# A planner's table of offsets, keyed by stream, segment and share of the work done

## Chip, core, metric

One core of one Trainium2 chip. The metric is device time per execution in microseconds, the median of the runs. The granted TensorE clock is 1.00 over the whole profile.

## What is computed

Two transformer layers over 2048 tokens of width 640, all in bf16: attention with a compressive memory (32 heads of 20 features, four segments of 512 tokens), then a feed-forward part (FFN) with 1728 hidden features. The second layer uses the same weights. Cut to what matters:

```python
for s in range(N):                                   # N = 4 segments, L = 512
    p = softmax(einsum('bhqd,bhkd->bhqk', qs, ks) * scale + mask)
    a_dot = einsum('bhqk,bhkd->bhqd', p, vs)
    a_mem = (phi(qs) @ M) / (phi(qs) @ z + 1e-06)    # memory of earlier segments
    outs.append(g * a_mem + (1.0 - g) * a_dot)       # g = sigmoid(beta)
    M = M + phi(ks)^T @ vs;  z = z + phi(ks).sum()
...
x = x + A(layernorm(x));  x = x + relu(layernorm(x) @ w1) @ w2      # twice
```

## The kernel before

The work is cut into eight stages, segment 0 to 7: layer a and segment s make segment 4a + s. A segment needs its tokens normalised (`lnorm`), transposed by a DMA on SP's queue (`turn`, L745) and projected: keys and queries (`proj_part`, evicted at L910 or L911), values (L965). Keys and queries go to a DRAM scratch (`spill`, L999) and come back laid out by head (`fill`, L1046, four transfers for each pair of head groups) into one of four `pad` buffers. A pair m of head groups (four heads each) then has ten half-rounds of scores (L1230, PE in quarters of rows), taken two at a time, ten exponentials on ACT (L1292), the causal mask on POOL (L1304), the product with the values, and the division by the softmax sums (L1376 to L1418). In segment 0 the product with the values is made token by token (L1363, 40 small matmuls on the whole array); afterwards it runs in quarters of columns (`apply`, L1324), is evicted (L1334) and transposed (`turn_pair`). The memory is read (`mem_read`, L1110) and written (`mem_write`, L1167), its keys transposed by `turn_k`; the segment's output is added up (`combine`, L1437), transposed (`turn_o`), multiplied by wo (`out_proj`) and added to x (L1446), and the FFN follows (`ffn`, `ffn_rest`, evicted at L1528 or L1529, added at L1550).

There are eight PSUM banks. The scores use two slots of two banks, all other groups four single banks. Until the last scores of segment 0, two of those four are lent to the scores as a third slot.

**What sets the order.** Each engine runs its instructions in the order in which they were recorded, and so does each DMA queue. A planner (`Sched.run`) fixes this order when the kernel is built. Every piece of work is a generator, a "stream", with a number n by the order in which it was added: 0 scores, 1 exponentials, 2 masks, 3 value products, 5 `turn_pair`, 6 `divide`, 7 `turn_o`, 8 and 9 the halves of `out_proj`, 10 and 11 the second normalisation, 12 `fill`, 13 `spill`, 14 `combine`, 15 and 16 phi, 17 and 18 `mem_read`, 19 `turn_k`, 20 `mem_write`, 21 to 26 and 28 the first tiles, 27 `proj_ln`, 29 and 30 the key and query projections, 31 the values, 32 and 33 the FFN, 34 the stores, 35 to 38 constants and loads; evictions are streams of their own with higher numbers. The planner keeps a model of when each engine is free and each ticket due. At each step it takes, of the streams' next operations, the one with the smallest key: the start by its model, plus a lateness term, plus the stream's entry in `SHIFT` in nanoseconds (line 348); ties go by priority, segment and n:

```python
key = (round(start + late + SHIFT.get((n, self.rank[id(st[1])]), 0)), 0.5 if op.urgent else prio, self.rank[id(st[1])], n)
```

A negative entry has an operation recorded ahead of others that would start a little sooner, a positive one behind them. `rank` is the segment for the streams made by `each` and 0 for all others, among them the scores, exponentials, masks, value products, pair transposes and divisions (made by `items` or by themselves). A group of matmuls (`group`, L702 and L705) is recorded on the whole array (L702) or in four quarters of columns (L705); the planner chooses after each score pair (`_mode`), by whether a value product, which runs in quarters of columns alone, is due within 2500 ns of its model.

Of the kernel before, what the change touches and what calls it, by code (L numbers as in the profile page):

```python
# [13 lines left out]
NSEG = 4  # L14
# [4 lines left out]
G = H // 4  # L19
# [139 lines left out]
class Spawn:  # L159
# [31 lines left out]
class Sched:  # L191


    def __init__(self, prog):
# [9 lines left out]
        self.landed = set()  # L204

# [7 lines left out]
    def set(self, *key, tks=()):  # L213
        assert key not in self.events, key
        self.events[key] = [t for t in tks if t is not None]

# [95 lines left out]
    def run(self):  # L312
        while True:
# [24 lines left out]
            for prio, n, st, alts, op, late in heads:  # L338
# [9 lines left out]
                key = (round(start + late + SHIFT.get((n, self.rank[id(st[1])]), 0)), 0.5 if op.urgent else prio, self.rank[id(st[1])], n)  # L348
# [33 lines left out]
            else:  # L382
# [6 lines left out]
                out = marks[0] if len(marks) == 1 else (marks or None)  # L389
# [53 lines left out]
def bass_interleave_layers__memory_aug_infini_attn__dense_activation_relu__prompt_kernel(  # L443
    nc, A_x, A_wq, A_wk, A_wv, A_wo, A_beta, B_x, B_w1, B_w2, out,
):
    with contextlib.ExitStack() as es:
# [649 lines left out]
        def mem_read(hb):  # L1096
            def f(a, s):
# [35 lines left out]
                if len(READ[a, s]) == 2:  # L1133
                    for p in range(2):
                        PHS[p].release(*READ[a, s])
# [538 lines left out]
```

## Time and profile before

| | |
|---|---|
| median of 3 runs | 553.89 us (553.56 to 554.15) |
| span of the profiled execution | 552.1 us; the other 1.8 us of the median lie outside the first and last instruction |
| PE busy | 544.5 us, 9969 matmuls |
| DVE, ACT, POOL busy | 417.5, 413.0, 195.8 us |
| exponentials of segment 0 | 19.1 to 60.3 us |
| exponentials of segment 1 | 69.3 to 123.0 us |
| exponentials of segment 7 | 420.2 to 475.5 us |

The profile of one execution gives busy times by engine and by stretch, the waits by who ended them, the chain of work that ended last, and a timeline in which instructions of one kind in a row are merged (start, length, engine, line, tiles, count, and in brackets the idle time ahead of it and what ended it). Matmuls are pipelined and their ends are modelled, so PE can be shown busy while it starts nothing new; the time from one start to the next shows that.

### The profile page before, as it was taken

The numbers are of one execution on the slowest core, as the hardware profiler recorded it, in microseconds if no ns is written. First come the engines' busy times: TensorE is split into PE (matmuls) and PEld (weight loads), VectorE is DVE, ScalarE is ACT, GpSimd is POOL, SyncE is SP. The second block draws the span as 40 slices with busy tenths as digits, with TensorE's granted clock in tenths as the row PEclk, the third lists the DMA queues.
The fourth block names the chain that finished last, engine by engine and source line by source line (L and its number), as shares of the span: only waits on it lengthen the run. The fifth ranks groups of instructions, "written<-read, shape, count | busy, mean of one in ns | idle before, by whom it ended". The sixth has DMA issues, their size and how long they took to land.

```text
span 552.1 us, 22367 instructions
## 1 busy us (share of the span) xinstructions
PE 544.5 (99%) x9969; PEld 311.6 (56%) x9969; DVE 417.5 (76%) x1052; ACT 413.0 (75%) x531; POOL 195.8 (35%) x305
## 2 busy tenths in 40 slices
PE   8999999999999999999999999999999999999998
PEld 7554554455554555646456465654646654766656
DVE  4977899899798949987788759987968788745102
ACT  6699779889878878788888858888887779423140
POOL 5345334333344334443434404444333434201000
PEclk9999999999999999999999999999999999999999
DMA  8596989623861533953377841359138521433101
GB/s 266 147 224 179 195 202 209 195 78 66 170 146 44 78 68 100 151 98 69 62 143 151 136 147 45 69 97 136 23 103 174 93 50 29 96 63 62 40 2 51
DMA packets 130163, 61.52 MB, mean 111 GB/s; under 512 B 108948, under 2 KB 119956, under 8 KB 130068
## 3 DMA queue, kind: packets, MB, share of 16 engines
q1 hardware_dynamic: 129504, 59.57, 50.4%
q8 instruction: 78, 1.28, 0.9%
q10 hardware_dynamic: 564, 0.53, 0.4%
q14 instruction: 17, 0.14, 0.1%
HBM read 20.56 MB, written 12.85 MB: 61 GB/s over the span
## 4 chain that ended last, share of the span: by engine, by line
PE 88%; ACT 6%; DMA 2%; DVE 2%; SPq 1%; issue 0%
PE ps L705 43%; PE ps L702 27%; PE ps L1230 9%; PE ps L1324 6%; ACT PT L1292 5%; PE ps L1110 2%; DMA wq_r<-in_A_wq_dram 1%; PE ps L1504 1%; DMA pad<-scr 1%; PE ps L1167 1%; DMA pad<-stg 0%; ACT stg L1075 0%; SPq L1026 0%; DVE stats L723 0%; DVE o_sb L1418 0%
## 5 line engine op out<-in xcount | busy, mean ns | idle before, releaser
L1292 ACT ACTIVATE PT<-ps 128x1024 bf16<-128x1024 f32 x320 | 308.8, 1032 | 55.9 <-PE ps L1230 53.9
L1304 POOL TENSOR_SCALAR_AFFINE_SELECT PT<-PT 128x512 bf16<-128x512 bf16 x256 | 169.0, 678 | 250.2 <-ACT PT L1292 250.2
L705 PE MATMUL ps<-xnT,w_r 128*32 128x512 bf16 x1464 | 89.1, 380 | 0.0
L705 PE MATMUL ps<-w_r,hT 128*32 128x320 bf16 (+1 forms) x1868 | 71.2, 295 | 0.0
L1230 PE MATMUL ps<-pad 20*128 20x512 bf16 (+3 forms) x1024 | 63.4, 301 | 0.8 <-DMA pad<-scr 0.3
L1550 DVE TENSOR_TENSOR x_sb<-x_sb,ps 128x320 bf16<-128x320 bf16 (+1 forms) x65 | 30.9, 475 | 43.6 <-PE ps L705 39.9
L702 PE MATMUL ps<-w_r,hT 128*128 128x320 bf16 x378 | 62.4, 300 | 0.0
L723 DVE BATCH_NORM_STATS2 stats<-x_sb 128x6 f32<-128x320 bf16 x124 | 55.2, 478 | 3.2 <-DMA x_sb<-in_A_x_dram 2.6
L705 PEld LDWEIGHTS ps<-xnT,w_r 128*32 128x32 bf16 x1464 | 36.0, 97 | 33.6 <-issue 4.4
L705 PEld LDWEIGHTS ps<-w_r,hT 128*32 128x32 bf16 x1868 | 47.5, 97 | 12.7 <-issue 0.2
L1529 ACT ACTIVATE hT<-ps 128x512 bf16<-128x512 f32 x55 | 33.0, 599 | 21.1 <-PE ps L705 19.6
L1230 PEld LDWEIGHTS ps<-pad 20*128 20x128 bf16 x1024 | 17.9, 92 | 53.1 <-ACT PT L1292 26.9
L1446 DVE TENSOR_TENSOR x_sb<-x_sb,ps 128x320 bf16<-128x320 bf16 x64 | 30.5, 481 | 19.3 <-PE ps L705 15.1
L702 PEld LDWEIGHTS ps<-w_r,hT 128*128 128x128 bf16 x378 | 34.8, 98 | 18.2 <-issue 5.3
L1324 PE MATMUL ps<-PT,v_aug 128*21 128x128 bf16 (+3 forms) x896 | 40.3, 300 | 0.0
L910 DVE CAST stg<-ps 128x512 bf16<-128x512 f32 (+1 forms) x41 | 27.3, 668 | 16.6 <-PE ps L705 9.5
L739 POOL TENSOR_TENSOR rstd<-lnU,mhalf 128x2 f32<-128x2 f32 (+2 forms) x27 | 21.1, 781 | 50.9 <-DVE lnU L735 43.4
L1528 DVE TENSOR_SCALAR hT<-ps 128x512 bf16<-128x512 f32 x49 | 33.5, 685 | 7.3 <-PE ps L705 6.0
L702 PE MATMUL ps<-xnT,w_r 128*128 128x512 bf16 x154 | 37.4, 380 | 0.0
L705 PE MATMUL ps<-wo_r,oT 128*32 128x320 bf16 x864 | 36.7, 300 | 0.0
L1334 DVE CAST otu<-ps 128x512 bf16<-128x512 f32 x45 | 30.7, 682 | 5.5 <-PE ps L1324 4.2
L1075 ACT ACTIVATE stg<-stg 128x512 bf16<-128x512 bf16 x50 | 31.7, 636 | 1.2 <-DVE rtmp L1073 1.0
(114 smaller groups left out, 741.3 us busy)
## 6 DMA issues: line engine op xcount, KB each, us to landing
pad<-scr SPq DMA_DIRECT2D x124, 80.0 KB
scr<-stg SPq DMA_DIRECT2D x34, 256.0 KB, 2.8
out_dram<-x_sb SPq DMA_DIRECT2D x15, 160.0 KB, 2.8
w_r<-in_B_w_dram SPq DMA_DIRECT2D x10, 216.0 KB, 2.6
w_r<-in_B_w_dram SPq DMA_DIRECT2D x13, 160.0 KB, 2.8
x_sb<-in_A_x_dram SPq DMA_DIRECT2D x10, 160.0 KB, 3.0
scr<-w_r SPq DMA_DIRECT2D x5, 256.0 KB, 3.2
wv_r<-in_A_wv_dram SPq DMA_DIRECT2D x1, 800.0 KB, 9.7
```

The source lines that it names most:

```text
L702: return e.matmul(view(dst.ap, b), a, b, start=(k == 0), stop=(k == last))
L705: return e.matmul(view(dst.ap[rows], b), part, b, start=(k == 0), stop=(k == last))
L723: tk = yield dve(320, 1, lambda e, c2=c2: e.bn_stats(stats6[:, t, c2, :], x_sb[:, t, c2 * 320:(c2 + 1) * 320]), xt)
L1075: te = yield act(512, lambda e, q=q: e.activation(q, q, ACT.Exp), [tr] + p, psum=False)
L1230: fns.append([(lambda e, z=z, j=j, hh=hh, N=N, o=o, sl=sl, q=hh % 2: e.matmul(slot.ap[:, q, o:o + N], sl.ap[32 * hh:32 * hh + DH, z, 0, 12 ...
L1292: tx = yield act(1024, lambda e, dst=dst, src=src: e.activation(dst, src, ACT.Exp, scale=SCALE), sc + pw)
L1304: tm = yield pool(600.0, lambda e, reg=reg: e.affine_select(out=reg, in_=reg, pattern=[[0, 4], [1, 128]], compare_op=ALU.is_ge, fill=0.0, ...
L1324: fns.append((lambda e, OD, j=j, hh=hh: e.matmul(OD.ap[32 * hh:32 * hh + DH + 1, 128 * j:L], VAUG[vx(a, s)][:, j, 4 * g + hh, :], pt.ap[:, ...
L1334: te = yield evac(L, 1, lambda e: e.tensor_copy(dst, OD.ap), lambda e: e.activation(dst, OD.ap, ACT.Copy), [tk] + OTU[0].tks)
L1528: th = yield evac(512, 1, lambda e: e.tensor_scalar(hT[:, dc, :], bk.ap[:, :], 0.0, None, ALU.max), lambda e: e.activation(hT[:, dc, :], b ...
L1529: lambda e: e.activation(hT[:, dc, :], bk.ap[:, :], ACT.Relu), [tk] + HT.tks)
L1550: ta = yield dve(n, 1, lambda e: e.tensor_tensor(x_sb[:, t, c0:c0 + n], x_sb[:, t, c0:c0 + n], bk.ap[:, 0:n], ALU.add), [tk], urgent=True)
```

## The change

The table `SHIFT` is replaced. Its key becomes a triple: stream number, segment, and a share of the stream's work in this segment (0 below 6 recorded operations, 1 below 20, 2 below 60, 3 from there). So that the streams that had no segment get one, `items`, `scores` and `exps` now tell the planner when they enter a segment (`enter`), and each recorded operation of a stream is counted (`made`). Streams that never enter a segment stay in 0. Instead of 86 offsets there are 229. The lists that gathered tickets until both halves of a piece of work were recorded become one helper, `meet`, that releases the same buffers with the same tickets. `rank`, the tie-break and the operations stay as they were.

```diff
@@ -172,18 +172,44 @@
 PE_MARGIN = 80.0
 HOLDERS = 1
 SHIFT = {
-    (5, 0): -3000, (7, 0): -700, (7, 1): 400, (7, 2): -1000, (7, 4): 4300, (7, 5): -1100, (7, 6): -2700,
...
-    (18, 1): -200, (18, 2): -100, (18, 3): -200, (18, 7): -400, (19, 0): -1600, (19, 1): 100, (19, 4): -100,
-    (19, 5): -400, (19, 6): 1000, (20, 0): -200, (21, 0): 200, (22, 0): 100, (24, 0): 100, (26, 0): -100,
-    (27, 4): 200, (27, 5): 200, (27, 6): -100, (27, 7): -100, (29, 6): -100, (29, 7): -400, (30, 6): -400,
...
-    (33, 5): -1400, (33, 7): -200, (34, 4): -800, (34, 7): -200, (36, 0): 100, (37, 0): 1500, (38, 0): -300,
+    (0, 0, 0): -138, (0, 0, 1): -25, (1, 0, 0): 200, (1, 0, 1): 200, (1, 0, 2): 200, (1, 1, 0): 700, (1, 1, 1): 700,
+    (1, 1, 2): 700, (1, 2, 0): -275, (1, 2, 1): -225, (1, 2, 2): -100, (1, 3, 0): -925, (1, 3, 1): -925,
+    (1, 3, 2): -925, (1, 4, 0): 500, (1, 4, 1): 525, (1, 4, 2): 500, (1, 5, 0): -1888, (1, 5, 1): -1888,
+    (1, 5, 2): -1888, (1, 6, 0): 100, (1, 6, 1): 100, (1, 6, 2): 100, (1, 7, 0): -1450, (1, 7, 1): -1450,
+    (1, 7, 2): -1450, (2, 0, 0): 400, (2, 0, 1): 400, (2, 0, 2): 1000, (2, 2, 0): 300, (2, 2, 1): 300,
...
+    (7, 3, 0): -375, (7, 5, 0): 7775, (7, 7, 0): 4500, (8, 1, 0): -200, (8, 1, 1): -200, (8, 1, 2): -150,
...
+    (12, 3, 1): -500, (12, 5, 0): -1525, (12, 5, 1): -1525, (12, 6, 0): -25, (12, 6, 1): -25, (12, 7, 0): 4500,
+    (12, 7, 1): 4500, (13, 0, 0): -513, (13, 1, 0): -700, (13, 2, 0): -300, (13, 3, 0): 300, (13, 4, 0): -2000,
...
+    (19, 0, 0): -850, (19, 1, 0): 700, (19, 2, 0): 200, (19, 4, 0): -700, (19, 5, 0): 4250, (19, 6, 0): 375,
+    (20, 0, 0): -162, (20, 0, 1): -162, (20, 1, 0): 25, (20, 1, 1): -188, (20, 4, 0): -600, (20, 4, 1): -1225,
+    (20, 5, 0): -125, (20, 5, 1): -125, (21, 0, 0): -25, (21, 0, 1): 100, (22, 0, 0): 400, (24, 0, 0): 188,
...
+    (27, 6, 0): -62, (27, 6, 1): -62, (27, 7, 0): -2075, (27, 7, 1): -112, (29, 1, 2): 50, (29, 6, 0): -175,
...
+    (34, 7, 0): 400, (35, 0, 0): -300, (36, 0, 1): -650, (37, 0, 0): -100, (37, 0, 1): -100, (38, 0, 1): -25,
 }
 HOLD_TOL = {"pe": 220.0, "act": 150.0, "dve": 200.0, "pool": 0.0, "sp": 0.0}
 
@@ -202,6 +228,10 @@
         self.mode = "full"
         self.soon = 0.0
         self.landed = set()
+        self.met = {}
+        self.seen = {}
+        self.phase = {}
+        self.made = {}
 
     def add(self, prio, gen):
         self.streams.append([prio, gen, None, None, False])
@@ -213,6 +243,21 @@
     def set(self, *key, tks=()):
         assert key not in self.events, key
         self.events[key] = [t for t in tks if t is not None]
+
+    def enter(self, gen, phase):
+        if self.phase.get(id(gen)) != phase:
+            self.phase[id(gen)] = phase
+            self.made[id(gen)] = 0
+
+    def place(self, n, gen):
+        k = self.made.get(id(gen), 0)
+        return n, self.phase.get(id(gen), 0), sum(k >= x for x in (6, 20, 60))
+
+    def meet(self, key, count, tks, then):
+        self.met.setdefault(key, []).extend(tks)
+        self.seen[key] = self.seen.get(key, 0) + 1
+        if self.seen[key] == count:
+            then(self.met[key])
 
     def _fill(self, st):
         while st[2] is None and not st[4]:
@@ -345,7 +390,7 @@
                 if not ok:
                     continue
                 end, start, k = min(ok)
-                key = (round(start + late + SHIFT.get((n, self.rank[id(st[1])]), 0)), 0.5 if op.urgent else prio, self.rank[id(st[1])], n)
+                key = (round(start + late + SHIFT.get(self.place(n, st[1]), 0)), 0.5 if op.urgent else prio, self.rank[id(st[1])], n)
                 if best is None or key < best[0]:
                     best = (key, st, end, start, k, op)
             if best is None:
@@ -387,6 +432,7 @@
                         self.t[(id(tk[0]), tk[1])] = end + tail
                         marks.append(tk)
                 out = marks[0] if len(marks) == 1 else (marks or None)
+            self.made[id(st[1])] = self.made.get(id(st[1]), 0) + 1
             st[2], st[3] = None, ((slot, out) if slot is not None else out,)
 
 
...
@@ -1129,11 +1175,12 @@
                     bk.release(tm)
                     wr.append(tm)
                 S.set("omem", a, s, hb, tks=wr)
-                READ.setdefault((a, s), []).append(tk)
-                if len(READ[a, s]) == 2:
-                    for p in range(2):
-                        PHS[p].release(*READ[a, s])
-                    BDS.release(*READ[a, s])
+
+                def read(tks):
+                    for slot in PHS + [BDS]:
+                        slot.release(*tks)
+
+                S.meet(("read", a, s), 2, [tk], read)
             return f
 
         def turn_k(a, s):
@@ -1205,7 +1252,7 @@
 
         HALVES = [(m, u, k) for m in range(NSEG * G) for u in range(5) for k in range(2)]
 
-        def scores():
+        def scores(me):
 
             pads = {}
             LEND_FROM, LEND_TO = ("stg", 0, 0, 4, 1), ("sc", NSEG * 0 + G // 2 - 1, 4, 1)
@@ -1262,6 +1309,7 @@
                         for z in (a, b):
                             fns += z[2][y] if y < len(z[2]) else []
                     return pe(233.0, fns, a[1] + b[1] + a[0].tks + b[0].tks, take=[a[0], b[0]], mode="rows"), None
+                S.enter(me[0], HALVES[h][0] // (G // 2))
                 tks = yield Either(ask)
                 for tk, sl in zip(tks, list(took)):
                     m, u, k = HALVES[h]
@@ -1270,8 +1318,9 @@
                         pads[m].release(tk)
                     h += 1
 
-        def exps():
+        def exps(me):
             for m in range(NSEG * G):
+                S.enter(me[0], m // (G // 2))
                 pts = []
                 for u, parts in enumerate(ROUNDS):
                     if u in (0, 2):
...
@@ -1511,9 +1555,7 @@
                             lambda e: e.activation(hR[:], bk.ap[:, 0:L // 2], ACT.Relu), [tk] + HT.tks)
             bk.release(th)
             S.set("hR", b, s, tks=[th])
-            HALF[b, s] = tk
-            if (b, s, 0) in HALF:
-                xt.release(tk, HALF[b, s, 0])
+            S.meet(("half", b, s), 2, [tk], lambda tks: xt.release(*tks))
 
         def ffn(b, s):
             xtk = yield Need("hx", b, s)
...
@@ -1589,6 +1629,7 @@
             def g():
                 for a, s in AS:
                     S.rank[id(me)] = NSEG * a + s
+                    S.enter(me, NSEG * a + s)
                     if early is not None:
                         for st in S.streams:
                             if st[1] is me:
@@ -1598,11 +1639,17 @@
             return me
 
         def items(f, count):
-            for n in range(count):
-                yield from f(n)
-
-        S.add(0, scores())
-        S.add(0, exps())
+            def g():
+                for n in range(count):
+                    S.enter(me, 2 * NSEG * n // count)
+                    yield from f(n)
+            me = g()
+            return me
+
+        for f in (scores, exps):
+            me = []
+            me.append(f(me))
+            S.add(0, me[0])
         S.add(1, items(causal, NSEG * G))
         S.add(1, items(apply, 2 * NSEG * G))
         S.add(1, each(free_v))
```

More of the change, by code (lines that the diff above doesn't have):

```diff
@@ L807, in first_tile, with both @@
             S.set("turned0", t, tks=[tc])
-            FIRST.setdefault(t // 2, []).append((tc, tT))
-            if len(FIRST[t // 2]) == 2:
-                bx.release(*[x for _, x in FIRST[t // 2]])
-                S.set("xt", 0, 0, t // 2, tks=[x for x, _ in FIRST[t // 2]])
-        FIRST = {}
+            def both(tks):
+                bx.release(*tks[1::2])
+                S.set("xt", 0, 0, t // 2, tks=tks[0::2])
+            S.meet(("first", t // 2), 2, [tc, tT], both)
         PIECES = ((0, 1), (1, 2), (2, 4))
@@ L1091, in phi_ @@
             return f
-        READ = {}
         early_done = []
@@ L1456, in turn_o @@
                 ot = yield Acq([OT[k]])
-                ot.users = []
                 tT = yield from turn(ot_sem[id(ot)], ot.ap, o_sb[:, 2 * k:2 * k + 2, :].rearrange(
@@ L1474, in f @@
                     if i % 2:
-                        ot.users.append(tk)
-                        if len(ot.users) == 2:
-                            ot.release(*ot.users)
+                        S.meet(("ot", a, s, i), 2, [tk], lambda tks, ot=ot: ot.release(*tks))
             return f
@@ L1490, in ln_b @@
             return f
-        HALF = {}
         def ffn_rest(b, s):
@@ L1540, in ffn @@
                 yield Spawn(6, square(dc, bk, tk))
-            HALF[b, s, 0] = tk
-            if (b, s) in HALF:
-                xt.release(tk, HALF[b, s])
+            S.meet(("half", b, s), 2, [tk], lambda tks: xt.release(*tks))
             w2t = yield Need("w2")
```

32 rows, old and new, of the table SHIFT are left out of this document.

## The prediction

> **What bounds the kernel now.** I read the busy times by stretch first, then PE's timeline inside the stretches that have holes, then the other engines' timelines beside those holes. The stretches (columns: length; busy us and instructions of PE, PEld, DVE, ACT, POOL; granted clock; DMA share; GB/s):
>
> ```profile
> 0.00:20.00 20.00, 17.47 (x165) 13.67 (x166) 11.91 (x38) 11.02 (x27) 8.16 (x26) 1.00 0.67 204
> 20.00:40.00 20.00, 19.60 (x249) 10.81 (x248) 17.20 (x45) 18.97 (x25) 9.32 (x14) 1.00 0.86 221
> 40.00:60.00 20.00, 18.57 (x292) 9.31 (x288) 15.40 (x44) 19.95 (x23) 11.83 (x18) 1.00 0.72 188
> 60.00:80.00 20.00, 19.26 (x181) 11.32 (x180) 17.04 (x50) 13.89 (x21) 5.99 (x9) 1.00 0.89 193
> 80.00:120.00 40.00, 40.00 (x587) 19.02 (x583) 36.44 (x88) 36.03 (x45) 16.66 (x26) 1.00 0.74 179
> ...
> 480.00:520.00 40.00, 40.00 (x1055) 27.25 (x1046) 18.90 (x51) 8.14 (x14) 1.52 (x2) 1.00 0.29 63
> ```
>
> PE has no hole after 80 us (0.13 us idle up to 480) at clock 1.00, and its last matmul starts at 549.5 of a span of 552.1. So a microsecond PE loses anywhere is late at the end, one for one, and only PE's time can be won. Only ahead of 80 us does PE stand idle, and there ACT is nearly full (38.92 of 40 us between 20 and 60).
>
> "Busy" hides part of the loss, since matmuls overlap. So I sum start-to-start times of PE's matmuls. Inside a group they are 215.5 ns for 512 columns and 136 ns for 320: 192 columns more cost 79.5 ns, 2.4 columns per ns, plus 2.5 ns each. Four matmuls on 32 columns or 20 rows each start together and count once. From first to last start 548.4 us pass. Of this, 491.2 us are columns; 37 us are 326 changes between the shapes (whole array, quarters of columns, quarters of rows), each 96 to 113 ns by the medians of its kind; 160 score pairs bring two each. The rest is small steps, the first 20 us, and stalls above the usual step: **4.3 us between 20 and 80 us, 0.6 us after 80**. How a stall looks (PE, start, length):
>
> ```profile
> 44.86 0.40 PE L1230 MATMUL ps<-pad 20*128 20x256 bf16 x8
> 45.19 0.60 PE L702 MATMUL ps<-hT,wk_r 128*128 128x512 bf16 x2
> 46.01 0.60 PE L702 MATMUL ps<-hT,wk_r 128*128 128x512 bf16 x2 [0.22 <-DVE o_sb L1380]
> ...
> 51.08 1.04 PE L702 MATMUL ps<-hT,wk_r 128*128 128x512 bf16 x4 [0.40 <-DVE w_r L910]
> 52.11 0.40 PE L1230 MATMUL ps<-pad 20*128 20x384 bf16 x8
> 52.57 1.15 PE L1363 MATMUL ps<-w_r,PT 128*128 128x21 bf16 x40
> 53.58 0.38 PE L702 MATMUL ps<-hT,wk_r 128*128 128x512 bf16 x1
> 53.95 0.40 PE L1230 MATMUL ps<-pad 20*128 20x256 bf16 x8
> 54.74 1.04 PE L702 MATMUL ps<-hT,wk_r 128*128 128x512 bf16 x4 [0.40 <-DVE w_r L910]
> ```
>
> Two matmuls from 45.19 are through the array at 45.62, the next starts at 46.01: 0.38 us lost, where the idle column says 0.22. The one at 54.74 waits for a PSUM bank. Of the group of five that holds it, four run at 51.08 and the fifth only at 53.58, behind a score pair and the 40 small matmuls of a value product (L1363); only then can DVE empty the bank:
>
> ```profile
> 52.57 0.17 DVE L735 TENSOR_SCALAR lnU<-mv 128x4 f32<-128x4 f32 x1
> 53.76 0.26 DVE L1376 RECIPROCAL rden<-ps 128x16 f32<-128x16 f32 x1 [1.02 <-PE ps L1363]
> 53.99 0.69 DVE L910 CAST w_r<-ps 128x512 bf16<-128x512 f32 x1
> ```
>
> DVE sat idle 1.02 us just before. So this is a fault of order alone, of the kind a table of offsets can cure. ACT was no help: it runs 14 exponentials without a gap from 43.7 to 56.6 us.
>
> **The change part by part.** No instruction is added or taken out; `meet` releases the same buffers on the same tickets as the lists it replaces, so it costs nothing. What moves is the recorded order, on all five engines and so in SP's DMA queue too, and through it which buffer is picked and which shape a group takes. 86 offsets, most tied to one segment, become 229; 53 of these are for the score, exponential, mask, value, transpose and divide streams, of which only the pair transposes had an offset (one, -3000, for the whole run). I cannot say from the diff which instruction passes which: one offset changes all later choices. So I bound each stage and choose.
>
> *20 to 80 us (segment 0 and the start of 1).* The 4.3 us are 1.24 us ahead of score pairs (10 of them) and 3.07 us elsewhere: 1.31 at three waits for a bank (46.0, 51.1, 54.7), 0.40 at 60.5 where the banks lent to the scores come back, 0.63 at 65.9 ahead of the memory update (L1167), and 0.73 in six smaller ones. Scores wait for a full ACT: I count no gain there. In segment 0 the exponentials get +200 and the scores -138 and -25, so that an ACT eviction due within 200 ns may go ahead of an exponential, and free a bank earlier. What this makes late is the exponentials of segment 0, covered by the 9.0 us between their end (60.3) and the first of segment 1 (69.3), in which PE lives on projections. No offset of the new table names the split groups themselves (the projections' streams have one of 50 ns in segment 1), so bank waits lie between 0 and 1.31 us won; I take two of the three, 0.9. The 60.5 and 65.9 waits (1.03; turn_k of segment 0 goes from -1600 to -850, phi gets new shares): taken at 0.7. The smaller six: 0.3.
>
> *After 80 us.* At most 0.62 us at four waits can be won; taken at 0.3. The memory update at 130.0 us runs on the whole array in 0.81 us where its sisters at 86.4 and 278.8 took 0.46 in quarters: 0.35 us, not counted.
>
> *First 20 us.* PE idles 2.53 us, 1.1 before the first instruction and 1.1 for the second weight's load, issued at 2.20 and landing at 8.85. The loads' offset falls from 1500 to -100, but they are issued one behind the other from 0.8 us already. Taken at nothing; above that at most 0.5 us.
>
> *The SP queue.* Offsets of 4500 to 7775 hold back turn_o in segments 5 and 7 (two transposes of 1.4 us each) and the last segment's pad fills (four transfers each). What lies beside them is PE's stock of FFN work. At the end the cover can be read: the last xnT transposes land at 510.2, and the FFN they feed begins at 519.8. The chain of attention may come 9.6 us later for nothing, and earlier for nothing too.
>
> Sum: 0.9 + 0.7 + 0.3 + 0.3 = 2.2 us less, a span of 549.9. The profiled execution's span is 552.1, and 1.8 us lie between it and the median of 553.89; I keep these, so **551.7**.
>
> The switches are the largest loss here (37 us). The Trainium skill (TensorEngine Tiling (Array Packing), Key Properties) states that a change of tiling mode drains the TensorE; the trace agrees, with 96 to 113 ns. That rule speaks against any change of order, which can add changes but hardly remove them; it stands as a rival below.
>
> **Rivals.**
> *No net effect* (553.9, within 0.2%, or 1.1 us, about what a measurement of this kernel can tell from no change): seven segments have nothing to win and hand back what segment 0 wins. It holds also if the new keys pick much the same order as the old. For it: 400 us of the span show no stall to cure.
> *PE waits in the later segments (slower).* PE is in order; a score pair recorded before its exponential has freed its bank stops everything behind it. Segment 0 loses 1.24 us on 20 pairs, 0.062 us a pair; the other 140 pairs lose 0.17 us together. New exponential offsets of +700, -925, +500, -1888 and -1450 in segments 1, 3, 4, 5 and 7 push at just this. At segment 0's rate 140 pairs lose 8.7 us, at half of it 4.35. It decides when it eats the gain: 2.2 / 0.062, so 35 pairs. Half the rate gives 553.9 - 2.2 + 4.35 = 556.0; the full rate 560.4. Against it: ACT has 12% free there, in segment 0 hardly 3%.
> *More shape changes (slower).* Apart from the pairs' 320, six changes at 96 ns bring PE from the whole array to quarters for a value product. The planner chooses the shape after each pair by whether such a product is due soon; with another order it can guess wrong for up to 56 products: 50 more, 4.8 us. 25 more give 2.4 us, and with the gain lost 556.3.
> *The whole of it.* All stalls after 20 us go (4.9 us): 549.0; with the 0.35 and 0.5 above, 548.1.
>
> **Chances.** Forecast 0.50 (549.5 to 552.7), the whole 0.08, no net effect 0.21, late scores 0.15, more changes 0.06. So faster by over 0.2% 0.58, within 0.21, slower 0.21. Range: from 549.0 to the half rate with ten more changes, 557.0.
>
> **What would show it.** Right: PE's busy time between 20 and 80 us rises from 57.43 towards 59, the waits of L702 for DVE w_r L910 and of L1167 shrink, after 80 us PE stays full, the exponentials of segment 0 still end near 60 us. The rivals: PE rows of L1230 that wait for ACT PT L1292 after 80 us; more rows that pass from L702 to L1324 without a score pair between. I am wrong if PE's holes ahead of 80 us stay, or if the last FFN begins with PE idle, which would mean the attention chain had slipped by over 9.6 us.

## The result, and the profile after

| | before | after |
|---|---|---|
| median, 21 executions each | 554.22 us (553.18 to 557.69) | 556.36 us (555.03 to 557.67) |
| span of the profiled execution | 552.1 us | 553.7 us |
| ratio after/before | | 1.0027, 95% interval 1.0014 to 1.0039 |

So the new table makes the kernel slower by 0.27%, 1.5 us, where 2.2 us less were forecast. (The two medians lie 2.1 us apart; the ratio is the figure that has an interval, and it is used below.) In the code of after the lines of before stand some 46 further down: L702, L705, L910, L1230, L1292, L1304, L1363 are now L748, L751, L957, L1277, L1341, L1353, L1412.

The busy times by stretch (columns as before):

```profile
0.00:20.00 20.00, 16.80 (x167) 13.04 (x168) 12.07 (x40) 11.35 (x28) 8.27 (x26) 1.00 0.66 204
20.00:40.00 20.00, 19.29 (x228) 10.36 (x226) 17.39 (x44) 17.92 (x22) 9.46 (x14) 1.00 0.79 203
40.00:60.00 20.00, 17.66 (x276) 8.77 (x275) 15.71 (x42) 19.42 (x22) 11.56 (x18) 1.00 0.79 201
60.00:80.00 20.00, 19.87 (x219) 12.12 (x219) 17.87 (x54) 15.83 (x24) 6.81 (x10) 1.00 0.96 192
80.00:120.00 40.00, 40.00 (x614) 18.72 (x611) 35.78 (x87) 36.31 (x47) 15.86 (x25) 1.00 0.78 183
160.00:200.00 40.00, 39.80 (x534) 20.29 (x533) 36.09 (x90) 33.02 (x43) 15.29 (x22) 1.00 0.45 69
360.00:400.00 40.00, 39.47 (x824) 22.75 (x824) 34.26 (x82) 30.66 (x43) 13.46 (x19) 1.00 0.44 69
480.00:520.00 40.00, 40.00 (x1040) 26.38 (x1041) 21.84 (x58) 11.20 (x18) 3.25 (x5) 1.00 0.29 63
```

Between 20 and 80 us PE is busy for 56.82 us, where 57.43 were the start and 59 the hope; only the stretch from 60 on gained. And PE no longer stays full after 80 us. PE's start-to-start times, added up as in the prediction, give the whole difference:

| us | before | after |
|---|---|---|
| columns | 491.14 | 491.21 |
| changes of shape | 34.15 (326) | 33.60 (321) |
| extra time until the clock is up | 2.38 | 1.82 |
| small steps | 12.98 | 12.98 |
| stalls, 0 to 20 us | 2.84 | 3.16 |
| stalls, 20 to 80 us | 4.31 | 4.79 |
| stalls after 80 us | 0.62 | 2.44 |

The sum of the differences is 1.6 us, as the spans have it; 1.82 us are lost in the part of the program that was full before, and the other lines take some of it back. (The prediction's 37 us of changes were too many: 326 of them at its own 96 to 113 ns are 31.3 to 36.8. "Until the clock is up": the profile has no clock row before 6.9 us in before and 4.7 in after, and until then matmuls of 128 columns start 107 ns apart, where 128 columns at 2.4 per ns are 53.) PE's waits, by who ended them:

```profile
PE ps L1277 <- ACT PT L1341: 1.4, 3, 0.7
...
PE ps L748 <- DVE w_r L957: 1.0, 1, 1.0
PE ps L751 <- DMA xnT<-xn_tok: 0.4, 2, 0.3
...
PE ps L1373 <- POOL PT L1353: 0.3, 1, 0.3
PE ps L1156 <- DVE om_sb L1171: 0.2, 1, 0.2
```

The first two lie ahead of 60 us, the last three after 80. PE from 52 to 58 us:

```profile
52.28 0.40 PE L1277 MATMUL ps<-pad 20*128 20x384 bf16 x8 [0.25 <-ACT PT L1341]
52.61 0.61 PE L748 MATMUL ps<-hT,wq_r 128*128 128x512 bf16 x2
53.05 1.16 PE L1412 MATMUL ps<-w_r,PT 128*128 128x21 bf16 x40
54.14 0.40 PE L1277 MATMUL ps<-pad 20*128 20x256 bf16 x8
54.47 0.82 PE L748 MATMUL ps<-hT,wq_r 128*128 128x512 bf16 x3
55.95 0.39 PE L1277 MATMUL ps<-pad 20*128 20x512 bf16 x4 [0.66 <-ACT PT L1341]
57.39 0.82 PE L748 MATMUL ps<-hT,wq_r 128*128 128x512 bf16 x3 [1.05 <-DVE w_r L957]
```

The three waits of 46.0, 51.1 and 54.7 us are gone. In their place a score pair waits for ACT twice (0.32 and 0.72 us by start-to-start), and a group for its bank 1.11 us. Over 20 to 80 us the stalls ahead of score pairs rose from 1.24 to 2.29 us (the third large one, 0.51, is at 26.7), the others fell from 3.07 to 2.50. For that last one, DVE beside it:

```profile
54.21 0.74 DVE L815 TENSOR_SCALAR xn_tok<-x_sb,mv,rstd 128x640 bf16<-128x640 bf16 x1 [1.13 <-POOL rstd L785]
54.88 0.24 DVE L1425 RECIPROCAL rden<-ps 128x16 f32<-128x16 f32 x1
55.04 0.82 DVE L815 TENSOR_SCALAR xn_tok<-x_sb,mv,rstd 128x640 bf16<-128x640 bf16 x1
55.78 0.59 DVE L1426 TENSOR_TENSOR rden<-rden,omg 128x16 f32<-128x16 f32 x1
56.30 0.43 DVE L815 TENSOR_SCALAR xn_tok<-x_sb,mv,rstd 128x640 bf16<-128x640 bf16 x1
56.66 0.68 DVE L957 CAST w_r<-ps 128x512 bf16<-128x512 f32 x1
```

The cast could have run when the group of 54.47 was through at 55.2; it stands behind three normalisations of segment 1 and a multiplication. The idle time of 1.13 us ahead of them, for `rstd` from POOL, is in the plan too. Their length is not: the planner has 0.35, 0.08 and 0.35 us for the normalisation of 55.04, the multiplication of 55.78 and the normalisation of 56.30, and the trace 0.82, 0.59 and 0.43 (the last section has the reason). With the normalisation of 54.21, 0.74 instead of 0.35, the cast begins 1.2 us later, against PE, than planned.

One wait after 80 us, PE and then POOL:

```profile
375.16 1.49 PE L751 MATMUL ps<-xnT,w_r 128*32 128x512 bf16 x24
376.90 0.72 PE L1373 MATMUL ps<-PT,v_aug 128*21 128x512 bf16 x16 [0.26 <-POOL PT L1353]
```

```profile
374.58 1.01 POOL L785 TENSOR_TENSOR rstd<-lnU,mhalf 128x4 f32<-128x4 f32 x1 [3.18 <-DVE lnU L781]
375.55 1.98 POOL L1353 TENSOR_SCALAR_AFFINE_SELECT PT<-PT 128x512 bf16<-128x512 bf16 x3
```

The value product is recorded half a microsecond behind the planned end of its mask, but POOL begins `rstd` 0.7 us later, against PE, than planned and takes 1.01 us for it, where the plan has 0.70: 0.45 us lost from start to start. The others are: 0.35 at 315.2 and 0.44 at 382.0 for a transpose (xnT), 0.25 at 254.6 for one (oT), 0.27 at 161.1 and 0.26 at 452.6 for a DVE eviction, 0.17 at 87.3 for a bank. No score pair waits after 80 us. At none of these places does the planner's own model, worked out from the kernel's code, have PE wait. It ends PE at 547.5 us with the old table and at 546.1 with the new: better in the model by 1.3 us, worse in the trace by 1.6. Nor does the new order cut it closer than the old: behind 80 us, 11 of 476 matmul operations that need a transfer stand within 1.0 us of its modelled landing (beyond the 0.14 us that it always keeps), in the old order 7; within 1.2 us it is 18 and 17. It is the model's costs that were too small. It leaves 0.8 to 1.0 us behind the three transposes of 254.6, 315.2 and 382.0 and has 3.91 us from issue to landing; in the trace these three take 5.18, 5.25 and 4.92. (All xnT transposes have a median of 3.82 before and 4.26 after, with one in ten at 5.0 or more in both.) Behind the two evictions and the bank it leaves 0.03 to 0.25 us.

None of this is the chance of one execution. The profiles of the kernels `new_cast`, `new_wide` and `head_old` below, which also run the new order behind 80 us, have waits at the same places (0.44 or 0.45 us at the mask, 0.38 to 0.42 at the transpose of 315.2). These four have 2.4 to 3.6 us of stalls behind 80 us in sum, the nine profiles with the old order there 0.2 to 0.8.

### The profile page after: what moved, and what is told of

It is laid out like the page before. It is cut to its first block, busy times and chain, and to the rows that moved or that the text cites. A ratio compares the mean times of both kernels' runs of the same rounds, so it can differ in the third digit from the quotient of the medians.

```text
span 553.7 us, 22668 instructions
## 1 busy us (share of the span) xinstructions
PE 543.9 (98%) x10119; PEld 309.9 (56%) x10119; DVE 419.4 (76%) x1052; ACT 413.6 (75%) x531; POOL 194.9 (35%) x305
## 4 chain that ended last, share of the span: by engine, by line
PE 76%; DVE 14%; DMA 6%; ACT 2%; SPq 1%; POOL 1%; issue 1%; DVEq 0%
PE ps L751 38%; PE ps L748 21%; PE ps L1277 7%; PE ps L1373 5%; DVE stats L769 2%; DVE xn_tok L815 2%; DMA xnT<-xn_tok 2%; PE ps L1156 2%; DMA x_sb<-in_A_x_dram 1%; ACT PT L1341 1%; DMA phk<-phs 1%; DVE phs L1123 1%; DMA oT<-o_sb 1%; DVE hT L1570 1%; POOL rstd L785 1%; PE ps L1548 1%
## 5 line engine op out<-in xcount | busy, mean ns | idle before, releaser
L1341 ACT ACTIVATE PT<-ps 128x1024 bf16<-128x1024 f32 x320 | 308.9, 1033 | 61.8 <-PE ps L1277 60.8
L1353 POOL TENSOR_SCALAR_AFFINE_SELECT PT<-PT 128x512 bf16<-128x512 bf16 x256 | 168.4, 676 | 257.5 <-ACT PT L1341 257.2
L751 PE MATMUL ps<-xnT,w_r 128*32 128x512 bf16 x1692 | 103.0, 380 | 0.0
L751 PE MATMUL ps<-w_r,hT 128*32 128x320 bf16 (+1 forms) x1812 | 70.2, 295 | 0.0
L1277 PE MATMUL ps<-pad 20*128 20x512 bf16 (+3 forms) x1024 | 63.4, 301 | 1.9 <-ACT PT L1341 1.4
L748 PE MATMUL ps<-w_r,hT 128*128 128x320 bf16 x392 | 64.4, 300 | 0.0
L751 PEld LDWEIGHTS ps<-xnT,w_r 128*32 128x32 bf16 x1692 | 41.3, 97 | 38.8 <-issue 4.8
L1571 ACT ACTIVATE hT<-ps 128x512 bf16<-128x512 f32 x52 | 31.1, 599 | 35.5 <-PE ps L751 34.6
L751 PEld LDWEIGHTS ps<-w_r,hT 128*32 128x32 bf16 x1812 | 45.0, 97 | 13.7 <-issue 1.6
L1277 PEld LDWEIGHTS ps<-pad 20*128 20x128 bf16 x1024 | 17.8, 92 | 54.6 <-ACT PT L1341 26.5
L748 PEld LDWEIGHTS ps<-w_r,hT 128*128 128x128 bf16 x392 | 36.3, 98 | 19.0 <-issue 5.4
L1570 DVE TENSOR_SCALAR hT<-ps 128x512 bf16<-128x512 f32 x52 | 35.3, 681 | 5.9 <-PE ps L751 4.9
L751 PE MATMUL ps<-wo_r,oT 128*32 128x320 bf16 x932 | 38.3, 300 | 0.2
L957 DVE CAST stg<-ps 128x512 bf16<-128x512 f32 (+1 forms) x42 | 28.0, 666 | 11.7 <-PE ps L751 6.7
L815 DVE TENSOR_SCALAR xn_tok<-x_sb,mv,rstd 128x640 bf16<-128x640 bf16 x60 | 31.2, 553 | 4.7 <-POOL rstd L785 4.7
L1383 DVE CAST otu<-ps 128x512 bf16<-128x512 f32 x41 | 28.1, 684 | 8.2 <-PE ps L1373 7.8
```

The lines of the kernel that those rows point to most:

```text
L748: return e.matmul(view(dst.ap, b), a, b, start=(k == 0), stop=(k == last))
L751: return e.matmul(view(dst.ap[rows], b), part, b, start=(k == 0), stop=(k == last))
L815: nm = lambda e, bx, t, k: e.tensor_scalar(bx.ap[:, k * D:k * D + D], x_sb[:, t + k, :], mv[:, t + k, 0:1], rstd[:, t + k:t + k + 1], ALU. ...
L1277: fns.append([(lambda e, z=z, j=j, hh=hh, N=N, o=o, sl=sl, q=hh % 2: e.matmul(slot.ap[:, q, o:o + N], sl.ap[32 * hh:32 * hh + DH, z, 0, 12 ...
L1341: tx = yield act(1024, lambda e, dst=dst, src=src: e.activation(dst, src, ACT.Exp, scale=SCALE), sc + pw)
L1353: tm = yield pool(600.0, lambda e, reg=reg: e.affine_select(out=reg, in_=reg, pattern=[[0, 4], [1, 128]], compare_op=ALU.is_ge, fill=0.0, ...
```

## The experiments

**Theories.** A: the loss is made behind segment 0, where the new order has PE wait for transposes, masks and evictions that come later than modelled. B: the loss is made in segment 0, by the waits at 52 to 58 us. While these ran a third came up, C: the new order's holes in segment 0 bring TensorE's clock down.

To cut an order in two, the planner's choice is replaced by a list: every stream's next operation is taken by its place in an order written out. With the order of before or after it records exactly that kernel's instructions.

```diff
-SHIFT = {
+ORDER = """
...
-                if best is None or key < best[0]:
-                    best = (key, st, end, start, k, op)
+                where, k, mode = left[0]
+                end, start, _, e = next(x for x in alts if x[2] == k)
+                if best is None or where < best[0]:
+                    best = (where, st, end, start, k, op)
```

**The two halves.** `head_new` has the order of after up to the first PE operation behind 64 us of the plan, then what is left in the order of before; `head_old` the reverse.

> The recorded order of the new table up to where PE reaches 64 us, from there the order of the old table for all that is left; no operation is changed. Theory A (the loss is in the later segments, where the new order leaves PE's matmuls less time behind transposes, masks and evictions: 1.8 us more of stalls after 80 us, against 0.3 to 0.7 us net in the head): 0.3 to 0.7 us over before, stalls after 80 us at some 0.6 us. Theory B (all of it starts in segment 0, and the later waits only follow from it): 1.5 us over before.

> The mirror of the run before: the old table's order up to 64 us, from there the new table's order for all that is left. Theory A: 0.8 to 1.7 us over before, with PE waiting for transposes and masks after 80 us as in the new kernel. Theory B: no difference from before (within 0.4 us).

Measured: head_new 554.82 us, ratio to before 0.9983 (0.9963 to 1.0004), stalls after 80 us 0.17; head_old 556.78, ratio 1.0034 (1.0006 to 1.0062), stalls after 80 us 3.10. The loss goes with the later part: A holds as to the place, B falls. (The 0.3 to 0.7 us over before that was expected of head_new didn't come.) PE's waits of head_old after 80 us (L1313, L908 and L1530 are the memory read, the matmuls in quarters and the value product there), where head_new's list is empty:

```profile
PE ps L1313 <- DVE x_sb L1652: 0.9, 1, 0.9
PE ps L908 <- DMA xnT<-xn_tok: 0.6, 2, 0.4
PE ps L1530 <- POOL PT L1510: 0.3, 1, 0.3
```

The second and third are those of after. The first, 1.00 us from start to start at 156.1, is not in after; 0.9 us or more would still lie between the halves without it. Ahead of 80 us head_old also has a wait of 1.03 us ahead of a score pair at 68.8, just behind the seam, that neither kernel has, though its stalls from 20 to 80 us are in sum no larger than after's. So the size is better read from the next run.

**Five operations later.** The order of after, with five of the PE operations that wait after 80 us recorded later, so that other matmuls go ahead. One of the five:

```diff
-30:c 30:c 16 30:c ... 13 0:r 30:f 16
+30:c 16 30:c ... 13 0:r 30:c 30:f 16
```

> The new kernel's order with five PE operations, those that stalled PE at 87, 161, 255, 315 and 453 us for 1.3 us in sum, recorded 0.35 to 0.55 us of PE work later; nothing else is moved by hand. Theory A: 1.0 to 1.3 us less than the new kernel, so 0.2 to 0.6 us over before. Rival (the waits are only passed on to the next operations, since what is late is a whole chain): less than 0.4 us gained, 1.1 us or more over before.

Measured: 555.24 us, ratio to before 0.9999 (0.9979 to 1.0019), 1.1 us below after's 556.36; stalls after 80 us 1.23 instead of 2.44. Half of the late waits and most of the loss go with five moves that touch nothing ahead of 80 us (22 more matmuls behind them go from the whole array to quarters of columns). But they work only in part as they were meant to. Of the five waits those at 87, 255 and 315 us are gone (0.77 us); those at 161 and 452 stay (0.27 and 0.25), and so does the mask's 0.45. The 0.44 at 382.0 went although nothing was moved there: its transpose landed in 3.51 us instead of 4.92. The last section has what the traces show of that.

**The fifth matmul.** The prediction's "fault of order alone" at 54.7 us of before, tried by itself: in the old order the fifth matmul of two groups goes ahead of the value product.

```diff
-0:r 27 3:f 3:f ... 3:f 27 29:f 1 38
+0:r 27 29:f 3:f 3:f ... 3:f 27 1 38
```

> The old kernel's order with two matmuls moved: the fifth of a group that stood behind the value product at 48.9 and at 52.6 us now runs ahead of it, so that its bank is emptied earlier. My prediction's claim (the stalls at 51.1 and 54.7 us are faults of order): 0.6 to 0.9 us less than before, the waits of these matmuls for DVE w_r gone. Rival (segment 0 is held by ACT, and PE only waits at its next score pair instead): within 0.3 us of before.

Measured: 554.70 us, ratio 0.9992 (0.9966 to 1.0019), which can't be told from before. The waits stay, 0.64 and 0.54 us from start to start (0.47 and 0.46 in before). PE (L1435 scores, L906 projections, L1570 values), then DVE:

```profile
52.03 0.39 PE L906 MATMUL ps<-hT,wk_r 128*128 128x512 bf16 x1
52.26 1.16 PE L1570 MATMUL ps<-w_r,PT 128*128 128x21 bf16 x40
53.43 0.40 PE L1435 MATMUL ps<-pad 20*128 20x256 bf16 x8
54.31 1.04 PE L906 MATMUL ps<-hT,wk_r 128*128 128x512 bf16 x4 [0.48 <-DVE w_r L1115]
```

```profile
53.45 0.26 DVE L1583 RECIPROCAL rden<-ps 128x16 f32<-128x16 f32 x1 [1.05 <-PE ps L1570]
53.62 0.63 DVE L1115 CAST w_r<-ps 128x512 bf16<-128x512 f32 x1
```

The fifth matmul now ends its group before the value product begins, and DVE still idles 1.05 us: the reciprocal that needs the value product is recorded ahead of the cast. The fault was in two queues, and I had read one. Moving the cast as well was not tried in the old order; in the new one it is, next.

**The cast.** The order of after, with the cast of 56.66 one operation ahead on DVE (`new_cast`); the same up to 80 us with the order of before behind (`head80_cast`); and one operation further ahead, before the multiplication of 0.59 us (`head80_c562`).

```diff
-27 30:f 1 30:f 3 2 27 27 30.2/1 1 0:r
+27 30:f 1 30:f 3 2 27 30.2/1 27 1 0:r          (new_cast, head80_cast)
+27 30:f 1 30:f 30.2/1 3 2 27 27 1 0:r          (head80_c562)
```

> The new order with one operation moved: on VectorE the cast that the group of query chunk 1 waits for (1.11 us of PE at 57.4 in the trace of after) is recorded ahead of the normalization that stood before it. Theory (the stall is a fault of the order on VectorE's queue): that stall goes, 1.1 us less; the picks of PSUM banks change with it, so a memory read near 155 us may wait 0.3 to 0.6; net 0.5 to 1.1 us below the new order at equal clock (554.4 to 555.0 where all at full clock), and fewer executions with a half-clock stretch, since the hole at 57.4 lies in the same 3.41 us as the one at 56.0. Rival (the group waits for something else just behind): a wait of 0.5 or more stays within 1 us of the old place.

> New order up to 80 us with the same cast ahead, old order from there. If the loss of the new order lies in its waits behind 80 us and in the cast's wait, this keeps what the new table gains up to 80 us and loses neither: late waits 0.2 to 0.6 us, no wait of 1.1 us at 57; median 552.8 to 553.8, below before (ratio 0.997 to 0.999). If the start of the new order is itself worse, or the old order behind it no longer fits (memory reads near 157 us that wait 1 us), 554.2 or above.

> As head80_cast, with the cast one more operation ahead on VectorE (ahead of the 0.60 us multiplication that stood between). Theory (the wait at 57.5 is VectorE's order): it shrinks from 0.76 to about 0.3, 0.4 to 0.5 us less, and the worst window there streams some 0.1 more, so fewer half-clock stretches; median 553.2 to 554.0. Rival (something behind it takes over, as it did in new_cast): 554.0 or above.

Measured: new_cast 556.86 us, ratio 1.0034 (1.0009 to 1.0058), a miss: the wait at 57 shrank from 1.11 only to 0.76, and the memory read waits 1.00 us at 156.8 where 0.3 to 0.6 was feared. head80_cast 554.17, ratio 0.9989 (0.9965 to 1.0013). head80_c562 554.49, ratio 0.9994 (0.9973 to 1.0016): the wait is down to 0.24, but that of the memory update (L1372), 0.85 in head80_cast and 0.28 in head_new, is 1.63.

```profile
PE ps L1372 <- DMA phk<-phs: 1.5, 1, 1.5
...
PE ps L906 <- DVE w_r L1115: 0.2, 1, 0.2
```

So this wait can be taken away by order, but in this trace the time is lost again at the next transfer: the transpose of phi's keys took 6.43 us to land, where head80_cast's took 5.75 and head_new's 4.88. With the switch to the old order at 90 us instead of 80:

> The same with the change to the old order at 90 us instead of 80: the waits behind 80 us come from where the two orders meet, so within 0.3 us of head80_c562, 553.2 to 554.2; 0.5 or more above it would say that the piece of the new order from 80 to 90 us costs by itself.

Measured: 554.43 us, ratio 1.0000 (0.9983 to 1.0018), as expected near head80_c562 (0.06 us below). No order that was tried beats before by more than the measurement can tell.

**The clock.** The list of executions gives each one's mean granted clock: 1.000, 0.997 where one stretch of 3.41 us ran at half clock, less where two or more did. Of before, 35 of 105 executions show at least one (three batches: 13, 14, 8 of 35), of after 16 of 21. After's 5 executions at full clock have a median of 555.47, the 16 others of 556.62. In before the two kinds lie further apart, by 2.3 to 3.2 us in the three batches, while 3.41 us at half clock can cost 1.7 at most (an estimate: half of 3.41); so something else goes with a fall of the clock there. Two executions of kernels with after's start were profiled with such a stretch, from 56.5 and 56.7 us (new_five_later, new_cast). The stretches of new_five_later (clock is the third number from the right):

```profile
49.64:53.06 3.42, 3.09 (x50) 1.58 (x50) 2.63 (x10) 3.42 (x6) 1.85 (x3) 1.00 0.78 231
53.06:56.47 3.41, 1.89 (x32) 0.75 (x28) 3.00 (x7) 3.41 (x5) 2.73 (x5) 1.00 0.57 153
56.47:59.88 3.41, 3.31 (x15) 0.97 (x16) 2.83 (x8) 1.44 (x2) 1.53 (x3) 0.50 0.90 205
```

The clock falls right behind the stretch with the holes, in which PE streams columns (columns by 2.4 per ns) for 0.34 of the time. To separate streaming from being busy, a pair: in the old order 50 matmuls of 8 columns, or 6 of 512, with zero weights (a tile that is unused until segment 1 is set to zero) go into an open group ahead of its fifth matmul. Both take 1.3 us of PE.

```diff
+                if (name, k) in EXTRA:
+                    tz = yield Need("zero")
+                    tz = yield pe(1300.0, [(lambda e, bk=bk, b=b, m=m: e.matmul(
+                        bk.ap[:, 0:8], zero, b[:, 0, 0:8], start=False, stop=False), m == EXTRA[name, k] - 1)
+                        for m in range(EXTRA[name, k])], tz)
```

> The old order, with 50 matmuls of 8 columns and zero weights put between the fourth and the fifth matmul of the group of query chunk 3 (they add zero to the open group; the output is unchanged), about 54 us into the span. PE is busy in them for about 1.3 us (50 at the 26 ns of a value product's 33-column matmul), but they stream only 0.17 us worth of columns. Clock theory (a stretch of 3.41 us in which TensorE streams columns for well under half the time is followed by 3.41 us at half clock): nearly every execution shows the half-clock stretch, where 13 of 35 of before do; the median is 1.3 us of added work plus some 0.8 to 1.5 us above before, 556.3 to 557.2. Rival (half clock strikes by chance, or depends on how long an engine is idle, not on what it streams): as old_wide, with some 4 in 10 of the executions at half clock, near 555.6.

> The same as old_thin at the same place, but with 6 matmuls of 512 columns and zero weights: again 1.3 us of PE (6 times 216 ns), now all of it streaming columns. The operations around it, and what waits for what, are those of old_thin. Clock theory: hardly an execution shows the half-clock stretch (0 to 2 in 10); the median is before at full clock plus 1.3 us, near 555.4, 0.8 to 1.8 below old_thin. Rival: no difference between the two beyond 0.3 us.

Measured: old_thin 556.57 us, 7 of 12 executions with a half-clock stretch, three of them with two or more; old_wide 555.52, 4 of 12, none with two. The medians differ as theory C has it (1.05 us). But C expected nearly all of old_thin's executions to fall and hardly one of old_wide's, and both counts miss that; 7 and 4 of 12 can be chance. The ratios to before, 1.0021 (0.9993 to 1.0049) and 1.0010 (0.9990 to 1.0029), overlap, and at full clock old_thin is the faster (554.40 against 555.39), which I can't explain. So the pair doesn't settle it. The trace of old_thin, its slowest execution, says more:

```profile
55.87:59.29 3.42, 3.42 (x106) 2.55 (x108) 1.32 (x5) 2.98 (x4) 2.58 (x5) 1.00 0.84 258
59.29:62.70 3.41, 3.14 (x17) 0.70 (x18) 2.69 (x7) 2.11 (x3) 1.74 (x4) 0.50 0.39 101
62.70:66.11 3.41, 3.41 (x31) 1.21 (x30) 1.59 (x3) 2.13 (x3) 1.02 (x2) 0.50 0.83 182
```

In the first row PE is busy for the whole 3.42 us (no two matmuls start more than 0.32 us apart), with the thin matmuls (8 columns each) and a value product (21 columns, not the 33 of the expectation); it streams for 0.40 of it, and the clock halves behind it for two stretches. old_wide's profiled execution has clock 1.00 at the same place. But the same trace had already fallen once, at 42.22, ahead of the thin matmuls and for another reason:

```profile
43.75 0.61 PE L1446 MATMUL ps<-pad 20*128 20x512 bf16 x4 [3.22 <-DMA pad<-scr]
```

PE waits 3.22 us for the fill of a `pad` buffer, and the stretch in which that begins streams 0.25. A late transfer can so cost its wait and the slower clock behind it, which may be what goes with the falls of before.

Then the fill in the new order itself, with four wide matmuls ahead of the wait at 56.0:

```diff
+        EXTRA = {((0, 1, 1, 1), 3): 4}
```

> The new order with 4 matmuls of 512 columns and zero weights put between the fourth and the fifth matmul of the group of query chunk 1, just ahead of the wait at 56.0 (they add zero; the output is unchanged). That is 0.86 us more work, of which 0.4 lies in the wait at 56.0; the group's bank comes free later, so the next group waits some 0.5 us longer. Clock theory: the worst 3.41 us of the stretch 53 to 58 no longer streams for only 0.33 to 0.43 of the time but for about 0.5, so the half-clock stretch there goes, and at most 5 of 12 executions show one (16 of 21 of after did); the median stays within 0.5 us of that of after although work was added (556.0 to 556.6), and at full clock it is 0.5 to 1.1 us above after's 555.5. Rival (the new order's half-clock share has nothing to do with this place): some 9 of 12 executions at half clock, median 557 or above.

Measured: 556.63 us, ratio 1.0029 (1.0009 to 1.0049), 0.27 above after although 0.86 us of work were added, and although its memory read waits 1.00 us at 156.5, as in new_cast and not in after. That fits C, but no more: in this kernel's profile the rows of the clock are missing, so its list, clock 1.000 in 12 of 12, can't be counted. (They are missing in head80_c562's profile too, whose list has three of 12 at 0.997; a 1.000 in any of these lists may be a missing record.) In the profiled execution no matmul is slowed after 50 us.

Executions of before fall to half clock too; no profile of before shows where. head80_cast's profile shows one early place: the stretch from 7.74 us, behind one in which PE streams 0.36, waiting for the first tiles. Twelve dummy matmuls instead of five in that wait:

```diff
-                yield pe(380.0, [(warm_mm, False) for _ in range(5)])
+                yield pe(750.0, [(warm_mm, False) for _ in range(12)])
```

> As head90_c562, with 12 instead of 5 dummy matmuls of 128 columns between the first and the second token tile's transposes at 6.7 us (0.37 us more at full clock, in a wait of 0.44; 0.75 more at half clock, 0.3 of it uncovered). Clock theory for the early half-clock stretch (about one execution in three of either order, in the stretch 5 to 9 us, streaming 0.30 to 0.38): 0.1 more streaming there, fewer half-clock stretches, mean 0.2 to 0.5 us lower; rival (the warm-up clock is free of this): no change, or 0.1 to 0.3 us slower by the uncovered part.

Measured: 555.15 us, ratio 1.0005 (0.9983 to 1.0027), 0.7 above head90_c562, with 3 of 12 at half clock where that kernel has none: a miss. Its profile has something else as well: the memory update waits 2.94 us for a transpose that takes 7.72 us to land, 1.36 and 6.14 in head90_c562.

## Why the prediction was wrong, step by step

- *PE sets the end, one for one.* Right: PE's account gives 1.6 us, the spans 1.6.
- *20 to 80 us, 1.9 us won.* Wrong: 0.48 lost. The waits that I took at 0.9 of 1.31 did go, all three; so did those taken at 0.7 of 1.03 (0.30 are left, at 68.0). Two steps failed. One I had set at nothing: "Scores wait for a full ACT: I count no gain there". It is 1.05 us of loss: PE's earlier matmuls meet an ACT that is full (14 exponentials in a row in before), and I asked only whether scores could gain. The other: the bank waits came back as one of 1.11 on DVE's queue. I had asked what is late next and named the exponentials; it was a cast, behind DVE operations that took longer beside POOL than the plan has them.
- *"A fault of order alone" at 54.74.* As I put it, not borne out: old_fifth mends PE's queue, and the wait stays, because DVE's queue has the same fault.
- *After 80 us, 0.3 won.* Wrong, and the largest term: 1.82 lost (head_old against head_new, new_five_later). The step that failed is "at most 0.62 us at four waits can be won": I counted which old waits could go, and put new ones, other than of score pairs, at nothing without a reason. The rival "PE waits in the later segments" had the place and the sign. Its mechanism and price were wrong: no score pair waits for an exponential there, and 4.35 to 8.7 us were priced. What waits are projections, value products, memory reads and output projections, for transposes, a mask and evictions, 0.2 to 0.5 us each, because these come later than the planner's costs say.
- *More shape changes.* Wrong sign: 321 instead of 326, 0.55 us won.
- *First 20 us at nothing; the SP queue covered.* Right: 0.32 more stalls against 0.56 less at the start, both of the size by which executions differ (the extra time until full clock is 1.5 to 2.4 us among the profiles); and PE is full from 480 to 520 us.
- *The clock.* Not in the sum at all: I read 1.00 in one profile as 1.00 in every execution. How much of the 1.5 us it makes up stays open. With falls in 33% of executions against 76%, it would be about 0.5 us at the 1.15 us between after's two medians, and nothing if before's rarer falls are charged with before's own 2.3 to 3.2. At full clock the loss is there too: 555.47 against 554.05 to 554.64 in the three batches of before, 0.8 to 1.4 us, and the profiles compared above are at full clock.

The time came out inside the range, on the side that I gave 0.21. What stays open: how much of the 1.3 us that the table gains in the planner's costs would be left with costs that fit the trace, and how often after falls to half clock at which of its two places, since one execution of each kernel shows where.

## What to carry to other kernels

A tuned order is only as good as the costs that it was tuned on: in front of an in-order engine, whatever takes longer than its modelled cost by more than the slack turns into a stall. So compare the model's cost of an operation with its length in the trace at the very place where the order puts it, and not by a median alone. Follow a wait through every queue that the releaser stands in, not only the one in which the fault is first seen. And where an engine is full, as ACT is in segment 0 here, taking away the waits around it can move them.

## What the runs showed of the hardware

*The clock halves without PE being idle.* In the profiles whose clock is recorded it changes on a grid of 3.41 us, whose phase differs by execution. Ahead of the end, when PE has no more work, the clock fell five times in these profiles, each time behind a stretch of this grid in which PE streamed columns for 0.40 of the time or less (0.25, 0.34, 0.36, 0.38, 0.40). Six others between 0.36 and 0.39 were not followed by a fall, and none above 0.40 was; so in these traces low streaming is not enough for a fall, but there was none without it. Past 20 us, the worst stretch of before's profile has 0.47 to 0.54, by the phase of the grid; that of after has 0.33 to 0.40 for six phases in ten. The Trainium skill (TensorE: Matmul & The Clock Gate, Part 1: The HAM clock gate (the "warmup" mystery)) tells of a free-running window of 3.4 us, and the grid agrees; its rule that the clock falls after an idle window does not cover old_thin, where PE was busy in all of it.

*DVE operations stretch beside POOL.* In after the multiplication on 128x16 elements at 55.78 takes 0.59 us and the normalisation of 55.04 takes 0.82; POOL's masks run from 55.05 to 56.35. Over the whole trace of after, the three such multiplications that lie wholly beside POOL's work take 0.32 to 0.60 us and the four that lie clear of it 0.15 to 0.18; of the normalisations, 14 beside POOL take 0.44 to 0.87 and 23 clear of it 0.43 to 0.45. The casts of 128x512 elements from PSUM take 0.67 to 0.69 either way. In head80_c562 the multiplication and a normalisation fall between two masks and take 0.16 and 0.43. DVE, then POOL:

```profile
55.31 0.68 DVE L1115 CAST w_r<-ps 128x512 bf16<-128x512 f32 x1
55.91 0.16 DVE L1584 TENSOR_TENSOR rden<-rden,omg 128x16 f32<-128x16 f32 x1
55.99 0.43 DVE L973 TENSOR_SCALAR xn_tok<-x_sb,mv,rstd 128x640 bf16<-128x640 bf16 x1
```

```profile
54.58 1.30 POOL L1511 TENSOR_SCALAR_AFFINE_SELECT PT<-PT 128x512 bf16<-128x512 bf16 x2 [0.27 <-ACT PT L1499]
56.41 1.30 POOL L1511 TENSOR_SCALAR_AFFINE_SELECT PT<-PT 128x512 bf16<-128x512 bf16 x2 [0.53 <-ACT PT L1499]
```

So the order on DVE also sets how long its operations take. The planner knows of this (it lengthens such an operation when it has POOL busy at its start), but it gave the three operations at 55 us 0.35, 0.08 and 0.35 us.

*Transposes take longer beside "instruction" transfers.* The profile lists DMA transfers of a kind that it calls "instruction", of 8 or 16 KB each behind 80 us. Of the 536 xnT and oT transposes that were issued behind 80 us in all fourteen profiles, 302 had such a transfer start within 3.4 us of their issue, and their median from issue to landing is 4.52 us; that of the 234 others is 3.52. Of the 81 that took 5.0 us or more, 72 are among the 302. In after 26 of 38 meet one, in before 20. All three transposes for which PE waits in after do, and in new_five_later, which issues its transfers in the same order, none of the three does: they land in 3.48, 4.44 and 3.51 us. The transfers of 377.06 in after and of 376.80 in new_five_later, each over 3.4 us:

```profile
q8 instruction: 1, 0.02, 1.8%
xnT<-xn_tok SPq DMA_TRANSPOSE x2, 4.7
...
xnT<-xn_tok SPq DMA_TRANSPOSE x2, 3.6
```

This is read from the traces; no run was made to test it, so whether the one causes the other is not shown.
